# Side work of experts 1 to 7 at other steps, layer 2 over four PSUM tiles, and the second expert's first rows fetched early

## The chip, the cores and the metric

The kernel runs on one core of a Trainium2 chip. Its time is the device time of one execution in microseconds (us); the number compared is the median of several executions. TensorE (PE in the profile) multiplies, VectorE (DVE) and ScalarE (ACT) read PSUM and work on SBUF, GpSimd (POOL) does element work and issues indirect DMAs, SyncE (SP) issues plain DMAs.

## The reference

```python
scores = scale * q @ k.T                      # 8 batches, 8 heads, 576 x 64
thresh = scores.max(-1) - tau                 # tau 0.02
attn = softmax(where(scores >= thresh, scores, -1e9)) @ v
x = attn.reshape(4608, 512)
noisy = x @ w_gate + log1p(exp(x @ w_noise)) * noise
top2 = the two largest of 8 per token; gates = softmax over them
for e in range(8):
    h = maximum(x[rows of e] @ w1[e], 0)      # 512 -> 1024
    out[rows of e] += gate * (h @ w2[e])      # 1024 -> 512
```

Everything is fp32. A matmul operand is split into a rounded high part and the rest (hi and lo), and each product is made of three matmuls (hi by hi, hi by lo, lo by hi).

## The kernel before

**Two halves.** The first 690 us or so are attention, batch by batch, with expert 0 started inside its end. Experts 1 to 7 follow, one after the other. The text is about them and about the seam between expert 0 and expert 1.

**Rows of an expert.** Gating writes, for each expert, a table of its tokens (up to 1188 slots, `slot_table`). An expert reads its table, gathers its rows from `x_rows` in blocks of 128 with indirect DMAs of POOL (`gather2`, L1155), writes each block back to a DRAM buffer `stage` (`bounce2`, SP, L1164), reads it in another layout with four DMAs (`load2`, SP, L1173, into two alternating buffers that the rows call n_zeros and n_xg), and turns it with four DVE transposes (`turn2`, L1182). `EARLY` gives expert 0 a table in two parts: the first 24 blocks of 32 slots hold tokens of batches 0 to 5 only and can be read before the last batches are gated.

**Two phases for an expert.** `PAIRS` cuts the slots into 640 (phase p=0) and 548 (p=1). Layer 1 is Strassen-like: for each of four column units u, seven products k, written here as (k,u), of six matmuls each (`product`, L1239), 28 products in a phase. They accumulate in three PSUM tiles for x, y, z, named by `bank1`: x is tp0 or tp1 by u's parity, y is tp2, z is tp3. `evict` empties them: copies on ACT (L1255), adds on DVE (L1258), then relu into hi (ACT, L1262) and lo (DVE, L1263). x of unit u is thus free again only after relu lo of (4,u), two units on.

**Layer 2.** p=0 has five `plain` tiles of 128 tokens (24 matmuls each, L1317, emptied by ACT L1308); p=1 has two plain tiles and `wide2`, four column parts c of 24 matmuls each (L1332), which DVE transposes out of PSUM (L1339). All take `self.bank(False)`, which rotates over four halves of two tiles of 1024 columns, sp0 and sp1, in the order sp0, sp1, sp0, sp1. Waits between engines are kept by whole tile, so two halves of one tile count as one.

**The order** is written by hand. `STEPS` lists the steps of PE in a phase: 28 products, two "old" steps (the end of the layer 2 before) and, from place 28 on, "new" steps, the first of its own layer 2; then the rest of layer 2. After each step come its evictions, then the side work listed for that step in `run`: `split1` (w1hi on ACT, L1125, w1lo on DVE, L1130) and `sum1` (POOL, L1113) make expert n's w1 operands, `w2hi` (ACT, L1139) and `w2lo` (DVE, L1144) those of w2, `turns` the row turns and loads, `sums` the differences of rows (DVE, L1193) and the split of the row operands X (ACT L1212, DVE L1217). w1, w2 raw values come by SP (L1103, L1135) into four buffers. Each engine runs its list in order.

**The seam.** `START` places expert 0's steps inside attention's last pairs. Its third group (`first[2]`, 14 blocks) and its wide2 run in `steps0`, where before also all of expert 1's first rows are gathered, bounced, loaded and turned, landing in `R0` (buffers qr0, qr1, xl).

Of the kernel before, what the change touches and what calls it, by code (L numbers as in the profile page):

```python
# [39 lines left out]
EARLY = (GROUPS[0] + GROUPS[1],)  # L40
# [8 lines left out]
NEW = ("B", "T", "t", "t5", "G", "Y", "q", "R0", "S", "X", "W", "V", "H")  # L49
# [678 lines left out]
class Experts:  # L728


    def __init__(self, tc, const, work, psum, state, w1, w2, out, x_dram, table, stage):
# [82 lines left out]
        for i, place in enumerate(("qr0", "qr1", "xl")):  # L814
            lay(("R0", i), place, 0, 512)
# [360 lines left out]
    def turn2(self, e, p, i):  # L1176
# [122 lines left out]
    def plain(self, e, t, col, m, order):  # L1299
# [3 lines left out]
        ps = self.bank(False)  # L1303
# [16 lines left out]
    def wide2(self, e, k, col, n, order, last):  # L1320
# [44 lines left out]
    def phase(self, e, p, side1, side2):  # L1365
        second = self.second_steps(e, p)
# [23 lines left out]
        assert not at, sorted(at)  # L1390

    def run(self, count):
        nc = self.nc
# [210 lines left out]
```

## Time and profile before

| what | us |
|---|---|
| median of 3 runs (range 1498.17 to 1506.39) | 1499.37 |
| the profiled execution | 1513.85 |
| its span, first to last instruction | 1512.1 |
| PE busy in it | 1424.1 (94%) |
| DVE, ACT, POOL busy | 1061.1, 856.1, 754.2 |
| mean granted TensorE clock | 0.983 of full |

The profiled execution is 1.0% above the median of the runs; 1.75 us of it lie outside the span. A row of the timeline gives start, length, engine, line, operation, tile written and tiles read, and in square brackets how long the engine had been idle and what ended that. A matmul row's length includes its pipeline tail: the next one starts before it ends, so what a matmul costs is the distance of two starts.

### The profile page before, as it was taken

To read this page: it belongs to the slowest core of one execution; us is meant where nothing else is said; L and a number is where in the kernel's file an instruction comes from. 1 tells how busy PE (TensorE), PEld (TensorE's weight loads), DVE (VectorE), ACT (ScalarE), POOL (GpSimd) and SP (SyncE) were. 2 spreads that over 40 slices of the span, in tenths; PEclk is the share of its full clock that TensorE was granted. 3 is DMA by queue.
4 is the path that set the end of the run, shared out by engine and by line. 5 is a ranking of instruction groups with operands and counts; after the bars stand their busy time and mean duration, and the time that the engine had idled before them with its cause. 6 is when DMAs were issued, how large, how long until landed. Compare 5 with 4: busy or idle time off the path is not lost.

```text
span 1512.1 us, 27923 instructions
## 1 busy us (share of the span) xinstructions
PE 1424.1 (94%) x9086; PEld 1159.8 (77%) x9086; DVE 1061.1 (70%) x2853; ACT 856.1 (57%) x1808; POOL 754.2 (50%) x1149
## 2 busy tenths in 40 slices
PE   8999999999999998989698999899898998998997
PEld 6776667676777766879588888888887887888885
DVE  7888888888888888634766657658658557666640
ACT  7888878888888886312445434435434434443441
POOL 4347565756565667234554444543543552552512
PEclk9999999999999999999899999999999999999999
DMA  7677677777777674346355556555554653663622
GB/s 197 184 195 186 194 180 195 180 204 177 207 178 190 139 211 140 75 109 167 104 128 153 146 99 169 126 117 140 129 142 111 147 135 97 153 153 79 139 29 31
DMA packets 189282, 220.60 MB, mean 146 GB/s; under 512 B 64212, under 2 KB 112300, under 8 KB 188112
## 3 DMA queue, kind: packets, MB, share of 16 engines
q1 hardware_dynamic: 161936, 178.91, 42.5%
q0 software_dynamic: 27200, 39.88, 15.3%
q8 instruction: 74, 1.21, 0.3%
q14 instruction: 72, 0.59, 0.1%
HBM read 103.25 MB, written 60.61 MB: 108 GB/s over the span
## 4 chain that ended last, share of the span: by engine, by line
PE 66%; DVE 10%; issue 9%; ACT 6%; DMA 4%; POOL 3%; SPq 1%; POOLq 0%; DVEq 0%; ACTq 0%
PE m_tp L1239 14%; PE m_sp L1317 13%; PE tp L397 11%; PE tp L331 9%; PE sp L283 9%; PE m_sp L1332 3%; PE m_sp L1000 2%; DVE n_pt L1130 2%; PE tp L417 1%; DVE n_p L1217 1%; DVE n_qr L1258 1%; DMA slot_table<-pay,sl 1%; PE tp L416 1%; POOL out L1021 1%; DMA out<-n_y,sx 1%
## 5 line engine op out<-in xcount | busy, mean ns | idle before, releaser
L296 ACT ACTIVATE e<-ns,nm 128x576 f32<-128x576 f32 x288 | 223.3, 776 | 43.2 <-DVE ns L294 34.3
L319 DVE SCALAR_TENSOR_TENSOR p<-ns,thr,e 128x576 f32<-128x576 f32 x256 | 221.8, 866 | 22.6 <-ACT thr L304 20.7
L294 DVE TENSOR_SCALAR_CACHE_REDUCE ns<-sp 128x576 f32<-128x576 f32 x288 | 214.3, 744 | 18.2 <-PE sp L283 13.0
L1021 POOL DMA_INDIRECT out<-n_y,sx x52 | 82.1, 1579 | 243.2 <-ACT n_y L1308 238.0
L331 PEld LDWEIGHTS tp<-ident,p 128*128 128x128 f32 x1024 | 110.3, 143 | 99.7 <-ACT ot L403 18.3
L334 ACT ACTIVATE pt<-tp 128x512 f32<-128x512 f32 x256 | 150.7, 589 | 55.6 <-PE tp L331 46.1
L397 PE MATMUL tp<-pt,vt 128*64 128x256 f32 (+1 forms) x1024 | 175.6, 427 | 0.0
L331 PE MATMUL tp<-ident,p 128*128 128x128 f32 x1024 | 167.6, 286 | 0.0
L283 PE MATMUL sp<-ks,qh 128*128 128x288 f32 x496 | 159.8, 336 | 5.4 <-DVE ns L294 4.8
L1258 DVE TENSOR_TENSOR n_qr<-m_tp,n_qr 128x320 f32<-128x320 f32 (+1 forms) x168 | 77.0, 461 | 115.2 <-PE m_tp L1239 103.7
L283 PE MATMUL sp<-ks,ql 128*128 128x288 f32 x496 | 138.4, 296 | 0.0
L1239 PE MATMUL m_tp<-n_p,n_pt 128*128 128x274 f32 (+1 forms) x700 | 117.0, 303 | 12.7 <-ACT n_qr L1255 8.1
L1255 ACT ACTIVATE n_qr<-m_tp 128x320 f32<-128x320 f32 (+1 forms) x168 | 67.7, 411 | 107.0 <-PE m_tp L1239 103.6
L213 POOL TENSOR_TENSOR lok<-kr,hik 128x640 fp32r<-128x640 f32 x31 | 56.9, 1834 | 140.5 <-ACT hik L212 139.2
L1239 PEld LDWEIGHTS m_tp<-n_p,n_pt 128*128 128x128 f32 x700 | 100.9, 188 | 19.4 <-ACT n_qr L1255 11.3
L1308 ACT ACTIVATE n_y<-m_sp,gw 128x512 f32<-128x512 f32 (+1 forms) x52 | 35.5, 685 | 130.2 <-PE m_sp L1317 102.7
L1021 POOL DMA_INDIRECT out<-n_y,ix x60 | 97.5, 1625 | 16.2 <-issue 13.3
L640 POOL DMA_INDIRECT slot_table<-pay,sl x80 | 88.2, 1102 | 33.7 <-DVE m_vt L881 16.5
L283 PEld LDWEIGHTS sp<-ks,qh 128*128 128x128 f32 x496 | 93.8, 189 | 7.7 <-DVE ns L294 5.1
L283 PEld LDWEIGHTS sp<-ks,ql 128*128 128x128 f32 x496 | 94.4, 190 | 0.0
L1239 PE MATMUL m_tp<-n_vt,n_pt 128*128 128x320 f32 (+1 forms) x364 | 89.4, 301 | 4.4 <-issue 3.3
L397 PEld LDWEIGHTS tp<-pt,vt 128*64 128x64 f32 x1024 | 56.7, 135 | 42.4 <-issue 27.8
(539 smaller groups left out, 3884.2 us busy)
## 6 DMA issues: line engine op xcount, KB each, us to landing
qh<-hiq SPq DMA_DIRECT2D x124, 144.0 KB
ql<-loq SPq DMA_DIRECT2D x124, 144.0 KB
n_raw<-w SPq DMA_DIRECT2D x56, 256.0 KB
kr<-k SPq DMA_DIRECT2D x32, 320.0 KB
out<-zeros SPq DMA_DIRECT2D x19, 512.0 KB
qr<-q SPq DMA_DIRECT2D x32, 288.0 KB
vt<-v SPq DMA_DIRECT2D x8, 1152.0 KB
n_zeros<-stage SPq DMA_DIRECT2D x140, 64.0 KB
```

What stands on the lines that cost most here:

```text
L283: nc.tensor.matmul(o, q_, k_, start=(i == 0), stop=(i == len(parts) - 1))
L294: nc.vector.tensor_scalar(ns, sp[:, :, 0:HALF], -1.0 / math.sqrt(D), None, op0=ALU.mult, op1=ALU.min, accum_out=nm)
L296: nc.scalar.activation(e, ns, AF.Exp, bias=nm, scale=-1.0)
L319: nc.vector.scalar_tensor_tensor(p, ns, thr, e, op0=ALU.is_le, op1=ALU.mult, accum_out=ssum[n][:, c:c + 1])
L331: nc.tensor.transpose(tp[:, kt, :], p[:, 128 * kt:128 * kt + 128], ident)
L334: nc.scalar.activation(pt[n][:, s, :, c0:c0 + 128], tp, AF.Copy)
L397: nc.tensor.matmul(o[64 * s:64 * s + 64, 0:c1 - c0], w, x, start=(kt == 0), stop=(kt == 4))
L640: st = nc.gpsimd.indirect_dma_start(out=table, out_offset=bass.IndirectOffsetOnAxis(ap=d["sl"][0:m, i, c:c + 1], axis=0), in_=d["pay"][0:m ...
L1021: st = self.nc.gpsimd.indirect_dma_start(out=out, out_offset=bass.IndirectOffsetOnAxis(ap=idx, axis=0), in_=y, in_offset=None, compute_op= ...
L1239: nc.tensor.matmul(ps[:, 0:n], w[a[0]][hw][:, 128 * (a[1] + c):128 * (a[1] + c) + 128], s[hx][:, c0 + c, t0:t0 + n], start=(first and i == ...
L1258: return lambda: nc.vector.tensor_tensor(to, ps, to, op=ALU.add)
L1317: nc.tensor.matmul(ps[0:m], x[:, col:col + m], y, start=(i == 0 and j == 0), stop=(i == 7 and j == 2))
```

## The change

1. `EARLY` holds for expert 1 too: its table also comes in two parts, and 768 of its slots are filled from batches 0 to 5. Its five first blocks are gathered, bounced and partly loaded and turned in `START` (new entries tok1, ix1, gd, bd, ld, td); `steps0` keeps only three turns, one load, the sums and w1. The `R0` buffers are gone; the rows land in buffers of expert 0's rows. This adds 5 DMAs to SP and 10 small instructions to DVE.
2. Layer 2 takes its tiles from a list, `spot`: sp, the other sp, tp2, tp3, sp, the other sp, the first 512 columns of each. x of unit u is tp0, tp1, sp{1-lead}, tp0 for u = 0 to 3.
3. Side work moves by some steps. The order of PE's steps, the matmuls and their number stay.

```diff
-EARLY = (GROUPS[0] + GROUPS[1],)
+EARLY = (GROUPS[0] + GROUPS[1],) * 2
...
+    gc=(16, 16, 16, 17), bc=(16, 16, 16, 17), lc=(17, 17, 18, 20), tc=(19, 20, 21, 22), tok1=-18, ix1=1,
+    gd=(1, 2, 18, 18, 19), bd=(3, 4, 19, 19, 20),
+    ld=(22, 22, 23, 23), td=(23, 23))
...
     def bank1(self, name, u):
-        place = {"x": f"tp{u % 2}", "y": "tp2", "z": "tp3"}[name]
+        place = {"x": ("tp0", "tp1", f"sp{1 - self.lead}", "tp0")[u], "y": "tp2", "z": "tp3"}[name]
...
+    def spot(self):
+        return self.arena[self.spots.pop(0)][:, 0:512] if self.spots else self.bank(False)
...
-            ps = self.bank(False)
+            ps = self.spot()
...
     def phase(self, e, p, side1, side2):
+        lead = self.lead
+        pair = [f"sp{lead}", f"sp{1 - lead}"]
+        self.spots = pair + ["tp2", "tp3"] + pair
...
+        self.lead = 1 - lead if p == 0 else lead
...
+            self.spots = ["sp0", "sp1", "tp0", "tp1", "sp0"]
...
-        for s, f in (rows(1, 0, (0, 0, 0, 3, 3), (2, 2, 3, 5, 6), (4, 4)) + turns(1, 0, (6, 7, 12, 13, 20), (6, 7, 13))
-                     + sums(1, 0, 21) + [(0, call(self.w1load, 1, 0))] + sum1(1, 0, 6) + split1(1, 0, (8, 9, 10))
+        for s, f in (turns(1, 0, (1, 1, 4), (1,), 2) + sums(1, 0, 6) + [(0, call(self.w1load, 1, 0)), (1, call(self.w1load, 1, 1))]
+                     + sum1(1, 0, 4) + split1(1, 0, (13, 14, 15))
...
-                s, v = [], (2, 6, 8, 11, 14, 17, 20, 23)
+                s, v = [], (4, 6, 11, 13, 18, 20, 25, 27)
...
-                + [(a + 2, call(self.w2load, e, 4 + i)) for i, a in enumerate(v[:4])] + turns(e, 1, (25, 27), (26, 29)),
-                turns(e, 1, (5, 7, 13), (6,), 2) + sums(e, 1, 14) + [(4, call(self.tokens, n, 0)), (30, call(self.index, n, 0))]
+                + [(a + 2, call(self.w2load, e, 4 + i)) for i, a in enumerate(v[:4])],
+                turns(e, 1, (1, 2, 8, 9, 15), (2, 3, 9)) + sums(e, 1, 16) + [(4, call(self.tokens, n, 0)), (30, call(self.index, n, 0))]
...
-                rows(n, 0, (1, 2, 3, 4, 5), (12, 13, 14, 15, 16), (18, 19)) + split1(n, 0, (9, 10, 13)) + sum1(n, 1, 12)
-                + [(16, call(self.w1load, n, 2))] + split1(n, 1, (17, 18, 20)) + [(22, call(self.w1load, n, 3))]
-                + sum1(n, 2, 22) + split1(n, 2, (25, 26, 28)) + sum1(n, 3, 30) + turns(n, 0, (25, 27), (26, 29)),
-                turns(n, 0, (5, 7, 13), (6,), 2) + sums(n, 0, 14) + split1(n, 3, (4, 5, 6))
-                + [(a, call(self.w2load, n, i)) for i, a in enumerate((8, 9, 14, 15))])
+                rows(n, 0, (1, 2, 3, 4, 5), (12, 13, 14, 15, 16), (18, 19)) + split1(n, 0, (6, 11, 13)) + sum1(n, 1, 13)
+                + [(16, call(self.w1load, n, 2))] + split1(n, 1, (18, 20, 25)) + [(28, call(self.w1load, n, 3))]
+                + sum1(n, 2, 22) + split1(n, 2, (27,)),
+                turns(n, 0, (4, 5, 9, 10, 15), (5, 6, 10)) + sums(n, 0, 16) + split1(n, 2, (None, 2, 3))
+                + sum1(n, 3, 4) + split1(n, 3, (7, 8, 11))
+                + [(a, call(self.w2load, n, i)) for i, a in enumerate((6, 6, 14, 14))])
```

Three places show how instructions stand now. First DVE in p=1 of an expert, from the relu lo of (4,2) (the first row) to that of (7,3) (the last row of each piece). The two L1258 rows are the adds of (3,3) and (7,3); n_pt are w1 lo parts, the four transposes one turned block of rows. The same functions stand 11 to 16 lines further down now. Before:

```order
L1263 SCALAR_TENSOR_TENSOR n_e_10156<-m_tp_9744,n_ns_10155 128x274
L1130 TENSOR_TENSOR n_pt_10166<-n_xl,n_pt_10166 128x512
L1130 TENSOR_TENSOR n_pt_10166<-n_nz,n_pt_10166 128x256
L1182 STREAM_TRANSPOSE n_kr_9895<-n_xg_9860 128x128
L1182 STREAM_TRANSPOSE n_kr_9897<-n_xg_9860 128x128
L1182 STREAM_TRANSPOSE n_hiq_9899<-n_xg_9860 128x128
L1182 STREAM_TRANSPOSE n_loq_9901<-n_xg_9860 128x128
L1258 TENSOR_TENSOR n_qr_9759<-m_tp_9801,n_qr_9759 128x274
L1263 SCALAR_TENSOR_TENSOR n_xr_10157<-n_qr_9759,n_xr_10157 128x274
L1130 TENSOR_TENSOR n_pt_10166<-n_raw_9767,n_pt_10166 128x512
L1258 TENSOR_TENSOR n_qr_9761<-m_tp_9769,n_qr_9761 128x274
L1263 SCALAR_TENSOR_TENSOR n_e_10159<-n_qr_9761,n_e_10158 128x274
```

Now:

```order
L1279 SCALAR_TENSOR_TENSOR n_e_10171<-m_sp_9049,n_ns_10170 128x274
L1274 TENSOR_TENSOR n_qr_9952<-m_tp_9885,n_qr_9952 128x274
L1141 TENSOR_TENSOR n_pt_10181<-n_raw_9813,n_pt_10181 128x512
L1279 SCALAR_TENSOR_TENSOR n_xr_10172<-n_qr_9952,n_xr_10172 128x274
L1274 TENSOR_TENSOR n_qr_9953<-m_tp_9798,n_qr_9953 128x274
L1279 SCALAR_TENSOR_TENSOR n_e_10174<-n_qr_9953,n_e_10173 128x274
```

Ahead of the add of (3,3) there stood two w1 parts and four transposes, and they are gone from there; one part and the relu lo of (3,3) stand between the two adds as before.

Second, DVE behind the last rows of that phase: the end of the X split (n_p, n_xr) and the transposes of wide2's parts c = 0 and 1 and 2 (L1339, now L1355). Before:

```order
L1217 TENSOR_TENSOR n_p<-n_loq_9901,n_p 128x640
L1217 TENSOR_TENSOR n_xr_9938<-n_qr_9759,n_vt_10035 128x640
L1339 STREAM_TRANSPOSE n_y_10659<-m_sp_9008 128x4x32
L1339 STREAM_TRANSPOSE n_y_10534<-m_sp_9008 128x4x32
L1339 STREAM_TRANSPOSE n_y_10572<-m_sp_9008 128x2x32
L1339 STREAM_TRANSPOSE n_y_10659<-m_sp_9033 128x4x32
L1339 STREAM_TRANSPOSE n_y_10534<-m_sp_9033 128x4x32
L1339 STREAM_TRANSPOSE n_y_10572<-m_sp_9033 128x2x32
L1339 STREAM_TRANSPOSE n_y_10659<-m_sp_9008 128x4x32
```

Now:

```order
L1355 STREAM_TRANSPOSE n_y_10674<-m_tp_9848 128x4x32
L1355 STREAM_TRANSPOSE n_y_10537<-m_tp_9848 128x4x32
L1355 STREAM_TRANSPOSE n_y_10583<-m_tp_9848 128x2x32
L1229 TENSOR_TENSOR n_p<-n_loq_9775,n_p 128x640
L1229 TENSOR_TENSOR n_xr_9978<-n_qr_9952,n_vt_9977 128x640
L1355 STREAM_TRANSPOSE n_y_10674<-m_tp_9885 128x4x32
L1355 STREAM_TRANSPOSE n_y_10537<-m_tp_9885 128x4x32
L1355 STREAM_TRANSPOSE n_y_10583<-m_tp_9885 128x2x32
L1355 STREAM_TRANSPOSE n_y_10674<-m_sp_9014 128x4x32
```

The parts c = 0, 1, 2 came out of two tiles, the third out of the first one's again; they come out of three. The last X parts stand behind c = 0 instead of ahead of it.

Third, SP behind expert 0's third group, where expert 1's blocks are loaded (stage is the DRAM buffer, n_raw, n_hik, n_lok are raw w1). Now:

```order
L1176 DMA stage<-m_p 128x512 x3
L896 DMA ti_76<-slot_table 32x26 x4
L900 DMA ti_76<-slot_table 4x2 x4
L950 DMA m_zeros<-stage 32x2x128 x4
L1185 DMA n_xg_9732<-stage 32x4x128 x4
L1185 DMA n_zeros<-stage 32x4x128 x4
L1185 DMA n_xg_9732<-stage 32x4x128 x4
L1185 DMA n_zeros<-stage 32x4x128 x4
```

Before, behind the same load of m_zeros, the last of expert 0's third group:

```order
L949 DMA m_zeros<-stage 32x2x128 x4
L1103 DMA n_raw_9765<-w 128x512
L1103 DMA n_raw_9767<-w 128x512
L1164 DMA stage<-n_qr_9759 128x512
L1164 DMA stage<-n_qr_9761 128x512
L1164 DMA stage<-n_xl 128x512
```

Three bounces of expert 1 moved ahead of that load, and its first four block loads follow at once.

## Rows read from the trace of the kernel before

**Rows 1.** The page, part 1: busy time, share of the span and instructions of each engine.

```profile
PE 1424.1 (94%) x9086; PEld 1159.8 (77%) x9086; DVE 1061.1 (70%) x2853; ACT 856.1 (57%) x1808; POOL 754.2 (50%) x1149
```

**Rows 2.** Busy time of each engine (instructions in brackets), granted clock, DMA share and GB/s in a stretch of one expert's length, from p=1 of expert 2 to p=1 of expert 3.

```profile
909.50:1018.60 109.10, 101.83 (x601) 91.76 (x600) 72.46 (x174) 47.16 (x101) 52.00 (x59) 0.98 0.55 132
```

**Rows 3.** What PE waited for in experts 1 to 7 (738 us to the end), by line waiting and line waited for: us in total, times, longest.

```profile
PE m_tp L1239 <- DVE n_qr L1258: 13.8, 7, 2.3
PE m_tp L1239 <- ACT n_qr L1255: 10.7, 15, 1.5
PE m_sp L1332 <- DVE n_y L1339: 10.5, 6, 1.8
PE m_tp L1239 <- DVE n_ns L1263: 5.0, 8, 0.8
PE m_tp L1239 <- issue: 4.3, 10, 0.8
PE m_tp L1239 <- DVE n_ptr L1263: 4.1, 8, 0.6
```

**Rows 4.** Timeline around (4,3) in p=1 of one expert: PE first, then DVE.

```profile
931.08 0.85 PE L1317 MATMUL m_sp<-n_pr,n_ns 128*128 128x512 f32 x3
934.18 0.39 PE L1239 MATMUL m_tp<-n_vt,n_xr 128*128 128x274 f32 x1 [2.24 <-DVE n_qr L1258]
...
930.04 0.50 DVE L1182 STREAM_TRANSPOSE n_kr<-n_xg 128x128 f32<-128x128 f32 x2
...
932.57 1.20 DVE L1130 TENSOR_TENSOR n_pt<-n_raw,n_pt 128x512 fp32r<-128x512 f32 x1
933.69 0.43 DVE L1258 TENSOR_TENSOR n_qr<-m_tp,n_qr 128x274 f32<-128x274 f32 x1
```

**Rows 5.** PE busy (instructions), granted clock, DMA share and GB/s in six stretches of 3.5 us, one in each of experts 1 to 6: the first, and the sum over the six.

```profile
826.00:829.50 3.50, 3.50 (x12) 0.53 0.00 0
...
sum 21.00, PE 21.00; mean PE 3.50
```

**Rows 6.** Timeline at wide2 of the same expert: PE at the start of c = 2, and DVE.

```profile
953.29 0.68 PE L1332 MATMUL m_sp<-n_qh,n_pt 128*128 128x292 f32 x3 [1.75 <-DVE n_y L1339]
...
947.96 0.82 DVE L1217 TENSOR_TENSOR n_p<-n_kr,n_p 128x640 fp32r<-128x640 f32 x1
948.69 0.82 DVE L1217 TENSOR_TENSOR n_p<-n_hiq,n_p 128x640 fp32r<-128x640 f32 x1
...
950.16 0.48 DVE L1193 TENSOR_TENSOR n_qr<-n_hiq,n_qr 128x320 f32<-128x320 f32 x1
950.57 0.48 DVE L1193 TENSOR_TENSOR n_qr<-n_loq,n_qr 128x320 f32<-128x320 f32 x1
...
952.60 1.16 DVE L1339 STREAM_TRANSPOSE n_y<-m_sp 128x128 f32<-128x128 f32 x6
```

**Rows 7.** Timeline of PE at the start of (1,3) in p=1.

```profile
922.79 0.53 PE L1239 MATMUL m_tp<-n_p,n_xr 128*128 128x274 f32 x2 [0.79 <-DVE n_ns L1263]
```

**Rows 8.** Timeline of the seam from expert 0 to expert 1: SP, DVE, PE.

```profile
713.08 0.84 SPq L1103 DMA_DIRECT2D n_raw<-w  x2
714.02 1.85 SPq L1173 DMA_DIRECT2D n_zeros<-stage  x4
...
720.82 0.50 DVE L1182 STREAM_TRANSPOSE n_kr<-n_zeros 128x128 f32<-128x128 f32 x2 [4.64 <-DMA n_zeros<-stage]
...
728.36 1.10 PE L1332 MATMUL m_sp<-m_qh,m_pt 128*128 128x292 f32 x3 [9.95 <-DVE m_y L1339]
```

**Rows 9.** Busy time of each engine, granted clock (behind the five engines), DMA share and GB/s in two stretches of the seam.

```profile
720.40:728.36 7.96, 0.00 (x1) 0.00 (x1) 7.54 (x17) 1.31 (x2) 3.60 (x4) 0.50 0.19 62
728.36:734.10 5.74, 5.74 (x23) 5.74 (x24) 5.67 (x9) 3.40 (x6) 0.00 (x0) 0.50 0.01 1
```

**Rows 10.** Timeline of the last block's load and turn in p=1 of two experts: SP's four issues and the first two of DVE's transposes.

```profile
936.94 1.73 SPq L1173 DMA_DIRECT2D n_zeros<-stage  x4
...
940.25 0.51 DVE L1182 STREAM_TRANSPOSE n_kr<-n_zeros 128x128 f32<-128x128 f32 x2 [0.46 <-DMA n_zeros<-stage]
...
1045.94 3.06 SPq L1173 DMA_DIRECT2D n_zeros<-stage  x4
...
1050.57 0.50 DVE L1182 STREAM_TRANSPOSE n_kr<-n_zeros 128x128 f32<-128x128 f32 x2 [1.78 <-DMA n_zeros<-stage]
```

**Rows 11.** Timeline at the start of a p=0: PE at (1,1), ACT's copy of it, PE at (6,1).

```profile
964.28 1.04 PE L1239 MATMUL m_tp<-n_p,n_pt 128*128 128x320 f32 x6
...
968.29 0.44 ACT L1255 ACTIVATE n_qr<-m_tp 128x320 f32<-128x320 f32 x1 [1.56 <-PE m_tp L1239]
...
968.78 0.41 PE L1239 MATMUL m_tp<-n_vt,n_pt 128*128 128x320 f32 x1 [0.82 <-issue]
```

**Rows 12.** Timeline of expert 0's third group: POOL's gather, SP's last load, DVE's turn and split, PE's first matmul on it.

```profile
659.60 0.98 POOL L929 DMA_INDIRECT m_p<-x_rows,sx  x1 [11.75 <-issue]
...
677.87 1.73 SPq L949 DMA_DIRECT2D m_zeros<-stage  x4
...
681.07 0.63 DVE L961 STREAM_TRANSPOSE m_loq<-m_zeros 128x64 f32<-128x64 f32 x4 [0.46 <-DMA m_zeros<-stage]
682.18 0.42 DVE L964 TENSOR_TENSOR m_xr<-m_loq,m_vt 128x256 fp32r<-128x256 f32 x1 [0.48 <-ACT m_vt L963]
...
687.97 0.35 PE L979 MATMUL m_tp<-m_vt,m_xr 128*128 128x420 f32 x1
```

More of the change, by code (lines that the diff above doesn't have):

```diff
@@ L48 @@
 PLACES = 4
-NEW = ("B", "T", "t", "t5", "G", "Y", "q", "R0", "S", "X", "W", "V", "H")
+NEW = ("B", "T", "t", "t5", "G", "Y", "q", "S", "X", "W", "V", "H")
 UNITS = range(4)
@@ L739, in __init__ @@
         self.xt, self.ht, self.wraw, self.wt, self.tok = {}, {}, {}, {}, {}
+        self.rows, self.held, self.spots = {}, {}, []
         self.spacer = const.tile([1, 1], F32, name="spacer1")
@@ L813, in __init__ @@
                 lay((n, i), place, 0, 512)
-        for i, place in enumerate(("qr0", "qr1", "xl")):
-            lay(("R0", i), place, 0, 512)
         lay(("S", 0), "xl", 0, 512)
@@ L1077, in start @@
         add(d["ix"], self.index, 0, 0)
+        add(d["tok1"], self.tokens, 1, 0)
+        add(d["ix1"], self.index, 1, 0)
+        for i in range(5):
+            add(d["gd"][i], self.gather2, 1, 0, i)
+            add(d["bd"][i], self.bounce2, 1, 0, i)
         for e, g, n in ((0, 0, "a"), (0, 1, "b"), (0, 2, "c")):
@@ L1080, in start @@
                 for i in range(2):
-                    add(d["tokb"][i], self.tokens, i, 1 - i)
-                    add(d["ixb"][i], self.index, i, 1 - i)
+                    add(d["tokb"][i], self.tokens, i, 1)
+                    add(d["ixb"][i], self.index, i, 1)
             for i in range(-(-GROUPS[g] // 4)):
@@ L1096, in start @@
                 add(d["l2"][i + 3 * g], self.store, 1)
+        for n, f in (("ld", self.load2), ("td", self.turn2)):
+            for i in range(2):
+                add(d[n][i], f, 1, 0, i)
+        for i in range(2):
+            add(d["ld"][2 + i], self.load2, 1, 0, 2 + i)
         return s
@@ L1146, in landing @@
     def landing(self, e, p, i):
-        return self.buf("R0", i % 3) if (e, p) == (1, 0) else self.buf("H", *((3, 0), (3, 1), (6, 0), (7, 0), (7, 1))[i])
+        return self.buf(*(("r0", 0), ("r0", 1), ("r", 1), ("r", 2), ("r", 0))[i]) if (e, p) == (1, 0) else self.buf("H", *((3, 0), (3, 1), (6, 0), (7, 0), (7, 1))[i])
     def gather2(self, e, p, i):
@@ L1154, in gather2 @@
         self.fresh = True
-        self.nc.gpsimd.indirect_dma_start(out=self.landing(e, p, i)[0:m, 0:512], out_offset=None, in_=self.x[0],
+        self.nc.gpsimd.indirect_dma_start(out=self.landing(e, p, i)[0:m, 0:512], out_offset=None,
+                                          in_=self.x[(e, p) == (1, 0)],
                                           in_offset=bass.IndirectOffsetOnAxis(ap=self.tok[e][2][0:m, t:t + 1], axis=0))
@@ L1390, in phase @@
         assert not at, sorted(at)
+        self.lead = 1 - lead if p == 0 else lead
     def run(self, count):
         nc = self.nc
-        self.rows, self.held, self.now, self.pending = {}, {}, 0, []
+        self.now, self.pending = 0, []
         def call(f, *a):
@@ L1399, in split1 @@
         def split1(e, u, s):
-            return ([(x, call(self.w1hi, e, u, n)) for x, n in zip(s, "asb")]
-                    + [(x + 1, call(self.w1lo, e, u, n)) for x, n in zip(s, "asb")])
+            return ([(x, call(self.w1hi, e, u, n)) for x, n in zip(s, "asb") if x is not None]
+                    + [(x + 1, call(self.w1lo, e, u, n)) for x, n in zip(s, "asb") if x is not None])
         def sum1(e, u, s):
@@ L1440, in run @@
         assert not at, sorted(at)
-        self.old = []
+        self.old, self.lead = [], 1
         for e in range(1, E):
```

11 lines of the change are left out of this document (5 added, 6 removed).

## The prediction

> **What bounds the kernel now.** The page first [rows 1]: PE is busy 94% of the span and the next engine, DVE, 70%, so what can be won lies in PE's holes and in stretches where its clock is not full. One expert of the steady part takes 109.1 us, with PE busy 101.8 and a mean clock of 0.98 [rows 2]. The table of PE's waits over experts 1 to 7 then says whom the holes wait for [rows 3]; see in it that four of the six lines name DVE, together 33.4 us in 29 waits, and that the other two (ACT's copy L1255, and "issue"), 15.0 us in 25 waits, are smaller and more scattered. The timelines say why DVE is late at each; the seam from expert 0 to expert 1 is one more and the largest hole [rows 8].
>
> **Part by part. The wait at (4,3) in p=1.** (4,3) adds onto the x of unit 3, so it waits until DVE has read it for (7,3). DVE does that at 933.69, because it came out of row transposes at 930.04 and then had a w1 part of 1.20 us ahead of the add; PE stands 2.24 us [rows 4]. The line is 13.8 us in 7 waits [rows 3]. In the new order two w1 parts and four transposes are gone from ahead of the adds. By such rows (0.50 us for two transposes, so some 0.8 for four that overlap; a part no shorter than the 0.43 of an add and no longer than 1.20) that is 1.7 to 3.2 us of DVE's queue, an estimate, as much as the hole, and PE has three layer 2 steps, 2.1 us, between (7,3) and (4,3). I take the wait as gone: 13.8 us. Nothing else was queued as late there: (7,3)'s copy on ACT is ahead of it.
>
> **wide2.** c = 2 stands 1.75 us until DVE has transposed c = 0 out of the same tile [rows 6]; 10.5 us in 6 waits [rows 3]. DVE is at the X split then (0.74 us each from row to row) and stays there in the new order; it even does c = 0 no sooner. But c = 2 goes to another tile whose last reader, ACT's eviction of a plain tile, is two parts back. Gone: 10.5 us. What is late next is the next phase's (2,0), which needs tp2, where c = 0 now is, only some 11 us later.
>
> **x of units 2 and 3.** (1,3) in p=1 waits 0.79 us for the relu lo of (4,1) [rows 7], and (1,2) in p=0 likewise for (4,0): 5.0 and 4.1 us [rows 3]. With unit 2 in an sp tile and unit 3 in tp0, the readers to wait for are a unit further back. Gone: 9.1 us.
>
> **The size of a hole.** The idle column is counted from the modelled end of the matmul ahead, which lies about 0.16 us beyond where the next would have started (0.39 long, 0.23 apart in layer 2). 29 waits by 0.16 are 4.6 us more. Holes together: 38.0 us.
>
> **The clock.** Behind these holes PE's clock was granted at half: six stretches of 3.5 us at 0.51 to 0.53 [rows 5], five behind (4,3), one behind a wide2 wait. 21.0 us of work at about half speed lose 10.3 us, against what full clock would do. [...] This is the softest term: the profiled execution is 14.5 us above the median, and these stretches may not stand in every run. Its bounds are 0 and 10.3.
>
> **The seam.** In wide2 of expert 0 PE stands 9.95 us, since DVE, ahead of the transposes of c = 0, waits 4.64 us for a block of expert 1's rows and then works off the sums [rows 8]. The clock falls to half meanwhile, and the 5.74 us of work behind run at 0.50 [rows 9], which loses 2.9. Now the five blocks are turned before the third group's layer 1 is through, and wide2's parts use four tiles. With the same sum rule that is 9.95 + 0.16 + 2.9 = 13.0 us. Against it stands POOL: two gathers of about 1.3 us now stand among the slot_table scatters that expert 0's third group waits for, and three bounces, which wait for three more gathers, stand on SP ahead of that group's last load. That load was issued at 677.87, turned at 681.07 and split by 682.6, and PE needed it at 687.97 [rows 12], so 5.4 us were to spare. The two gathers cost 2.6, the bounces 1.5 of issue and 0 to 3 of waiting: 4.1 to 7.1 in all, so 0 to 1.7 us late. I take 1.
>
> **New waits on DVE.** In p=1 blocks 2 to 4 are turned 4 or 5 steps of 0.7 us behind their loads, where 7 to 9 stood between before. From the first of four issues to the turn it took 3.3 us at 936.94 and 4.6 at 1045.94, with DVE idle 0.46 and 1.78 [rows 10]. In p=1 the last load also stands behind two loads of w2 of 256 KB. DVE may so be 1 to 3 us late before the sums. What it has to do from there to the last X part that product (2,0) needs is one turn 0.8, six differences and two more of 0.41, six splits of 0.74 and c = 0's transposes 0.6, together 9.1 us. PE has 96 matmuls of 0.135 us less two steps, (1,0), and an old step until then, 13.5. The cover is 4.4 us, so I cost this at nothing; if it is gone, PE stands at (2,0). For p=0 more layer 2 lies behind (24 matmuls of 0.23 for each of three tiles). The moved w1 and w2 splits have one answer each: all are still ahead of their first product by a unit. I allow 3 us for small things in seven experts, between 0 and 8.
>
> Here the Trainium skill speaks against the change. In the trace a block's load issued right behind w1 loads (713.08, then 714.02) reached DVE at 720.82 [rows 8], 6.8 us from its first issue against 3.3 to 4.6 [rows 10]. "DMA: Bandwidth & Descriptors", section "Queues, rings and completion order", says that each DMA engine consumes the descriptors of one ring in order, so a small load behind large ones of the same queue waits for theirs. That row agrees with it; by it the last load of p=1 would be late by more than my 1 to 3 us, and the sum would be that of the first rival.
>
> **The sum.** 38.0 + 10.3 + 13.0 - 1 - 3 = 57.3 us off the profiled execution's 1513.85: 1456.6. In the ratio of the median to it (1499.37 / 1513.85) that is 1442.6; I say 1443. The 15.0 us of the other two lines of rows 3 I leave in: at the start of a p=0, ACT's copy of (1,1) starts 3 us after PE's last row of it, with ACT idle, and (6,1) starts behind it [rows 11]; nothing in the change touches that.
>
> **The rivals.** First, slower: the rows of the next expert land late at each seam, as they did at the seam of expert 0. Place: the fifth block in p=1, its load behind two w2 loads, DVE waiting for it with X's split and wide2's transposes behind. It decides from 4.4 us later than the hand sum; below that nothing is lost. The price of the one case seen is 9.95 us of hole and 2.9 of half clock, 12.9; at six seams 77: 1499 - 57 + 77 = 1519. For it: the 4.64 us wait, and a turn now nearer its load. Against it: 4.4 us of cover by the hand sum, where expert 0's seam had the transposes right behind the turn. 4%.
>
> Second: PE's late signals. With the holes closed, PE arrives sooner at places like (6,1) where ACT learned of a finished product 3 us late. If two such waits of about 0.9 us are added in each of 13 phases, 23 us of the gain are lost: 1466. For it: it stands beside POOL's gathers, which stay. Against it: these waits don't follow the holes but the start of a phase. 13%.
>
> Third: the seam gives nothing, since expert 0's third group is late by what the new gathers and bounces cost and PE's clock falls there. Then the 13.0 are gone and some 5 more: 1461. 12%.
>
> Fourth: the change doesn't do what it says, because the profiled holes are mostly the profiler's and runs without it have few. Then little moves, about 1495. Against it: 94% busy and 7 equal holes in 7 experts. 3%.
>
> Fifth: the 15.0 us left in go as well, in part: 1432. 5%.
>
> **How the numbers follow.** The forecast has the rest, 63%: 1443, from 1435 (no small losses) to 1453 (no clock term). The range reaches to the fifth case below and the second and third above, 1430 to 1467, which holds 93% by these cases; I leave it so, since the clock term and the third case could come together. A measurement of this kernel tells about 0.5%, 7.5 us, from no change. Faster by more than that: 0.63 + 0.13 + 0.12 + 0.05 = 0.93. Within: 0.03. Slower: 0.04.
>
> **What would show it.** In the profile after: no DVE line above 1 us in total among PE's waits, for products or for wide2; mean clock of an expert at 1.00 where it was 0.98; an expert in about 101.5 us instead of 109.1; wide2 of expert 0 without a hole; DVE idle for block loads in p=1 by 1 to 3 us without PE standing at (1,0) or (2,0). Wrong I am if PE stands at (2,0) of a p=0, or if the two remaining lines grow by over 10 us.

## The result and the profile after

The changed kernel takes **1443.51 us** (median of 4 runs, 1442.19 to 1447.06), beside 1500.69 for the kernel before (4 runs, 1498.17 to 1506.39): a ratio of 0.9618, 95% interval 0.9584 to 0.9651. The forecast was 1443. The profiled execution took 1442.19 us (span 1440.5), which is 1.3 us below its median, where that of before was 14.5 us above. So the two traces differ by 71.66 us, and the medians by 57.2.

The page of the changed kernel, part 1, answers to [rows 1]:

```profile
PE 1401.6 (97%) x9086; PEld 1149.0 (80%) x9086; DVE 1044.8 (73%) x2863; ACT 856.8 (59%) x1808; POOL 756.1 (52%) x1149
```

Busy time by stretch follows (columns as in rows 2): a stretch of experts 2 and 3 as in [rows 2], and all of experts 1 to 7, from their first product to their last matmul. After:

```profile
870.00:970.00 100.00, 99.03 (x604) 90.94 (x603) 70.36 (x174) 47.22 (x102) 52.26 (x59) 1.00 0.61 144
729.40:1430.40 701.00, 692.94 (x4175) 632.04 (x4176) 467.96 (x1160) 322.62 (x693) 356.01 (x396) 1.00 0.58 135
```

Experts 1 to 7 in the kernel before:

```profile
738.30:1502.00 763.70, 714.08 (x4177) 639.79 (x4176) 482.46 (x1157) 323.70 (x693) 351.76 (x394) 0.99 0.52 124
```

The work of one expert (some 600 instructions of PE) now takes 100 us and not 109. Over seven experts the stretch is 62.7 us shorter. PE's idle time in it fell from 49.6 us (763.70 less 714.08) to 8.1, which is 41.6; its busy time fell by 21.1, and the granted clock rose to 1.00. The rest of the 71.66 lies ahead: expert 1's first product starts at 729.38 instead of 738.31, 8.9 us earlier.

What PE waited for from 690 us to the end after the change (us in total, times, longest), to be held against [rows 3]:

```profile
PE m_tp L1255 <- ACT n_qr L1271: 6.0, 8, 1.8
PE m_tp L980 <- ACT m_vt L964: 2.4, 1, 2.4
PE m_tp L1255 <- DVE n_y L1355: 2.0, 4, 0.7
PE m_tp L1255 <- DVE m_y L1355: 1.2, 1, 1.2
```

All four DVE lines of rows 3 are gone. A new one, 2.0 us in 4 waits, has come. ACT's line and "issue" together are down from 15.0 to 6.0; about 1.0 of that fall are six waits of 0.16 to 0.18 us at (1,3), x of unit 3, that rows 3 have under "issue".

DVE itself waits more than before. Its waits for blocks of rows over experts 1 to 7 (us in total, times, longest), after:

```profile
DVE n_kr L1194 <- DMA n_zeros<-stage: 63.5, 26, 7.3
...
DVE n_kr L1194 <- DMA n_xg<-stage: 19.7, 11, 2.6
...
DVE n_kr L1194 <- DMA ti<-slot_table: 7.8, 2, 4.1
```

The same of the kernel before:

```profile
DVE n_kr L1182 <- DMA n_zeros<-stage: 31.1, 13, 6.7
```

That is 83.2 us in 37 waits, and 91.0 in 39 with the last line, instead of 31.1 in 13: those two waits also stand ahead of the turn of a block (the fourth of a p=0), and the profile puts them down to another DMA. In each p=1 of experts 1 to 6 DVE now waits 4.7 to 5.5 us for blocks, where it was 0.5 to 1.8; the rest is in p=0. The timeline of one p=1 of the changed kernel (the expert after that of rows 4) shows where: SP's issues of the last three blocks and the loads of w2 among them (n_raw), DVE's turns of those blocks and its transposes of c = 0 and 1 of wide2, then PE at (5,0), the product behind (2,0).

```profile
1012.02 2.72 SPq L1185 DMA_DIRECT2D n_zeros<-stage  x4
1014.84 1.83 SPq L1185 DMA_DIRECT2D n_xg<-stage  x4
1016.77 0.95 SPq L1146 DMA_DIRECT2D n_raw<-w  x2
1017.82 1.82 SPq L1185 DMA_DIRECT2D n_zeros<-stage  x4
...
1016.38 0.51 DVE L1194 STREAM_TRANSPOSE n_kr<-n_zeros 128x128 f32<-128x128 f32 x2 [2.04 <-DMA n_zeros<-stage]
...
1020.20 0.51 DVE L1194 STREAM_TRANSPOSE n_kr<-n_xg 128x128 f32<-128x128 f32 x2 [2.02 <-DMA n_xg<-stage]
...
1023.09 0.51 DVE L1194 STREAM_TRANSPOSE n_kr<-n_zeros 128x128 f32<-128x128 f32 x2 [1.42 <-DMA n_zeros<-stage]
...
1030.92 0.63 DVE L1355 STREAM_TRANSPOSE n_y<-m_tp 128x128 f32<-128x128 f32 x3
...
1032.19 0.81 DVE L1229 TENSOR_TENSOR n_xr<-n_qr,n_vt 128x640 fp32r<-128x640 f32 x1
1032.92 0.63 DVE L1355 STREAM_TRANSPOSE n_y<-m_tp 128x128 f32<-128x128 f32 x3
...
1033.61 0.56 PE L1255 MATMUL m_tp<-n_p 128*128 128x320 f32 x2 [0.73 <-DVE n_y L1355]
```

DVE stands 2.04 + 2.02 + 1.42 = 5.48 us in this phase. The three blocks are turned 4.4, 5.4 and 5.3 us behind their first issues (rows 10 had 3.3 and 4.6). PE stands only 0.73 us for it: (5,0) writes tp3 and starts 0.06 us after DVE has read c = 1 out of tp3 (1032.92 + 0.63).

The seam, to be held against [rows 8, 9, 12]: timeline of the changed kernel with a gather of expert 1's rows on POOL, SP's last load for expert 0's third group, DVE's turn of it, PE's wait for that group and PE at expert 1's first product.

```profile
676.63 1.05 POOL L1166 DMA_INDIRECT m_p<-x_rows,sx  x1 [4.15 <-DMA stage<-m_p]
...
684.27 2.02 SPq L950 DMA_DIRECT2D m_zeros<-stage  x4
...
688.74 0.62 DVE L962 STREAM_TRANSPOSE m_loq<-m_zeros 128x64 f32<-128x64 f32 x4 [8.17 <-DMA m_zeros<-stage]
...
689.86 0.72 PE L980 MATMUL m_tp<-m_vt,m_xr 128*128 128x420 f32 x1 [2.36 <-ACT m_vt L964]
...
729.38 0.56 PE L1255 MATMUL m_tp<-n_p 128*128 128x320 f32 x2 [1.20 <-DVE m_y L1355]
```

The 9.95 us in wide2 are gone. The third group's last load is issued 6.4 us later than before (684.27 against 677.87), so PE stands 2.36 us for it, and 1.20 at expert 1's first product.

### The profile page after: what moved, and what is told of

Same layout as the page of the kernel before. It is cut to its first block, busy times and chain, and to the rows that moved or that the text cites. A ratio compares the mean times of both kernels' runs of the same rounds, so it can differ in the third digit from the quotient of the medians.

```text
span 1440.5 us, 27937 instructions
## 1 busy us (share of the span) xinstructions
PE 1401.6 (97%) x9086; PEld 1149.0 (80%) x9086; DVE 1044.8 (73%) x2863; ACT 856.8 (59%) x1808; POOL 756.1 (52%) x1149
## 4 chain that ended last, share of the span: by engine, by line
PE 60%; DVE 11%; DMA 9%; issue 8%; POOL 5%; ACT 4%; SPq 2%; POOLq 0%; DVEq 0%; ACTq 0%
PE m_tp L1255 13%; PE tp L399 9%; PE m_sp L1333 9%; PE tp L333 8%; PE sp L285 7%; PE m_tp L1333 5%; DMA slot_table<-pay,sl 2%; PE m_sp L1255 2%; DMA n_zeros<-stage 2%; POOL out L1022 1%; SPq L1185 1%; DMA kr<-k 1%; DVE n_pt L1141 1%; PE tp L419 1%; PE m_sp L980 1%
## 5 line engine op out<-in xcount | busy, mean ns | idle before, releaser
L321 DVE SCALAR_TENSOR_TENSOR p<-ns,thr,e 128x576 f32<-128x576 f32 x256 | 222.5, 869 | 22.4 <-ACT thr L306 21.1
L1022 POOL DMA_INDIRECT out<-n_y,sx x52 | 86.0, 1655 | 187.9 <-ACT n_y L1324 180.4
L215 POOL TENSOR_TENSOR lok<-kr,hik 128x640 fp32r<-128x640 f32 x31 | 57.3, 1848 | 140.1 <-ACT hik L214 139.7
L1274 DVE TENSOR_TENSOR n_qr<-m_tp,n_qr 128x320 f32<-128x320 f32 (+1 forms) x154 | 69.8, 460 | 50.4 <-PE m_tp L1255 49.8
L1255 PE MATMUL m_tp<-n_p,n_pt 128*128 128x320 f32 (+1 forms) x616 | 101.3, 301 | 0.5 <-ACT n_qr L1271 0.5
L1255 PEld LDWEIGHTS m_tp<-n_p,n_pt 128*128 128x128 f32 x616 | 88.9, 188 | 1.9 <-ACT n_qr L1271 1.1
L1271 ACT ACTIVATE n_qr<-m_tp 128x320 f32<-128x320 f32 (+1 forms) x140 | 57.6, 413 | 44.4 <-PE m_tp L1255 29.3
L1324 ACT ACTIVATE n_y<-m_sp,gw 128x512 f32<-128x512 f32 (+1 forms) x36 | 24.8, 688 | 96.9 <-PE m_sp L1333 67.7
L1224 ACT ACTIVATE n_vt<-n_qr 128x640 fp32r<-128x640 f32 (+1 forms) x42 | 29.3, 701 | 87.5 <-DVE n_qr L1205 87.5
```

The lines of the kernel that those rows point to most:

```text
L321: nc.vector.scalar_tensor_tensor(p, ns, thr, e, op0=ALU.is_le, op1=ALU.mult, accum_out=ssum[n][:, c:c + 1])
L1022: st = self.nc.gpsimd.indirect_dma_start(out=out, out_offset=bass.IndirectOffsetOnAxis(ap=idx, axis=0), in_=y, in_offset=None, compute_op= ...
L1255: nc.tensor.matmul(ps[:, 0:n], w[a[0]][hw][:, 128 * (a[1] + c):128 * (a[1] + c) + 128], s[hx][:, c0 + c, t0:t0 + n], start=(first and i == ...
L1274: return lambda: nc.vector.tensor_tensor(to, ps, to, op=ALU.add)
```

## The experiments

Three series, each on one chip; each kernel is compared with the kernel before in its own series, since that took 1516.66 us in the first (e1 to e4), 1523.82 in the second (e5 to e8) and 1501.76 in the third (e9 to e12).

**The kernel before once more** (no edit). 

> The kernel before once more, for a second trace. By the prediction's terms DVE's four lines among PE's waits stand again at 33 us within 2, since they follow from the order; what the first profiled execution had over the median (14.5 us) lies elsewhere, in the waits for ACT and issue and in attention. By the fourth rival the DVE lines are much smaller in an execution near the median, under 20 us.

One run: 1519.21 us. PE's waits for DVE stand there again: 13.5 us in 6 for L1258, 10.5 in 6 for wide2, 4.9 and 4.1 for the relus. So the holes of rows 3 belong to the program and not to one execution of it. The half clock behind them does less so: four stretches of 3.4 us in experts 1 to 7 here, two behind (4,3) and two behind a wide2 wait of 1.75 us, where [rows 5] had six.

**The PSUM tiles alone**, put into the kernel before with its old steps:

```diff
-        place = {"x": f"tp{u % 2}", "y": "tp2", "z": "tp3"}[name]
+        place = {"x": ("tp0", "tp1", f"sp{1 - self.lead}", "tp0")[u], "y": "tp2", "z": "tp3"}[name]
...
-            ps = self.bank(False)
+            ps = self.spot()
...
+        self.spots = pair + ["tp2", "tp3"] + pair
```

> The kernel before with the PSUM places of the change alone (spot, lead, bank1). If the terms add: the holes of wide2 and of the x tiles go, 10.5 + 9.1 and 2 of tails, and part of expert 0's wide2 hole, 3 to 7: 25 to 29 us less than before, and the (4,3) hole of 2.2 us with its half clock stays. If instead DVE is simply late and PE waits at the next place for it: 5 to 12 us less, with new DVE holes at the phase starts.

1490.20 us, ratio 0.9838 (0.9794 to 0.9881). PE's waits (columns as above):

```profile
PE m_tp L1244 <- DVE n_qr L1263: 16.5, 6, 2.8
PE m_tp L1244 <- ACT n_qr L1260: 14.7, 23, 1.8
PE m_tp L1244 <- DVE m_y L1344: 11.5, 1, 11.5
```

wide2 and the relu lines are gone, (4,3) has grown from 13.5 to 16.5, and the seam's hole has only moved, from wide2 to expert 1's first product, where it is 11.5 us. So the tiles take away two of the three causes and leave the third, which is one of order.

**The new steps alone**, with the old PSUM tiles:

```diff
-                + sum1(n, 2, 22) + split1(n, 2, (25, 26, 28)) + sum1(n, 3, 30) + turns(n, 0, (25, 27), (26, 29)),
-                turns(n, 0, (5, 7, 13), (6,), 2) + sums(n, 0, 14) + split1(n, 3, (4, 5, 6))
+                + sum1(n, 2, 22) + split1(n, 2, (27,)),
+                turns(n, 0, (4, 5, 9, 10, 15), (5, 6, 10)) + sums(n, 0, 16) + split1(n, 2, (None, 2, 3))
+                + sum1(n, 3, 4) + split1(n, 3, (7, 8, 11))
```

(and the other lists of experts 1 to 7 as in the change). 

> The kernel before with the side work of experts 1 to 7 at the new steps alone. If the terms add: the (4,3) hole goes, 13.8 and 1 of tails, and five of six half clock stretches, 8.6: 21 to 25 us less than before; wide2 and x holes stay, wide2's as long or some tenths longer, and one half clock stretch may now stand behind wide2. If DVE is simply late: 5 to 10 us less, with wide2's holes over 3 us.

1535.17 us, ratio 1.0123 (1.0085 to 1.0161): **slower**, by 1.2%. PE's waits:

```profile
PE m_sp L1332 <- DVE n_y L1339: 38.4, 6, 6.8
PE m_sp L1332 <- DVE m_y L1339: 12.5, 2, 10.8
PE m_tp L1239 <- DVE n_ptr L1263: 9.5, 14, 0.9
...
PE m_tp L1239 <- DVE n_qr L1258: 1.7, 5, 0.4
```

The order does what was forecast at (4,3): 13.5 us have become nothing, for the 1.7 us of that line stand at (4,0). But wide2's wait has grown from 10.5 to 38.4 us, again in 6 waits: DVE comes to the transposes of c = 0 later, because it waits for the last blocks, and PE's third part needs the tile that c = 0 stands in.

**The early fetch alone**, with the old steps of experts 1 to 7 and the old tiles:

```diff
-EARLY = (GROUPS[0] + GROUPS[1],)
+EARLY = (GROUPS[0] + GROUPS[1],) * 2
...
+    gd=(1, 2, 18, 18, 19), bd=(3, 4, 19, 19, 20),
+    ld=(22, 22, 23, 23), td=(23, 23))
```

> The kernel before with the early fetch of expert 1's rows alone (EARLY, START, steps0). By the sum of the prediction 12 us less, of which the trace of the changed kernel showed 9 between the first matmul of expert 0's second half and expert 1's start; by the third rival nothing or 5 us more. In the steady part nothing changes: one expert 109 us.

1522.42 us, ratio 1.0035 (1.0017 to 1.0053): 5.8 us slower. PE's waits for the end of expert 0:

```profile
PE m_sp L1348 <- DVE m_y L1355: 5.3, 1, 5.3
...
PE m_tp L980 <- ACT m_vt L964: 3.0, 1, 3.0
```

The hole in wide2 is halved and not gone, since c = 2 still waits for c = 0, and PE stands 3.0 us for the third group. That group starts 6.0 us later than in e1 (698.14 against 692.19), and from there to expert 1's first product only 4.1 us are won. Alone, with the old tiles and the old order, the early fetch gives nothing.

**The change again, in the second series** (no edit). 

> The changed kernel on the chip of this job. If its gain is the interaction seen between the parts (PSUM places alone about 25 us less, order alone about 18 more, early fetch alone about 5 more), the whole is again 3.5 to 4.5% under the kernel before of the same job, although its parts alone sum to about nothing. Its DVE again waits 80 us for block loads in experts 1 to 7 (31 in the kernel before).

1462.81 us, ratio 0.9594 (0.9556 to 0.9632). The ratio holds; the waits don't all. ACT's copy is 13.4 us in 20 waits here, against 6.0 in 8 above: in each p=1 of experts 1 to 6 PE stands 0.6 to 1.1 us at (6,1) and twice 0.4 after it, where the first trace has one wait of 0.4 or none. The new DVE line is 2.7 in 5, four at (5,0) and one of 0.26 at (2,0). One stretch of 3.4 us at half clock stands in expert 1, behind a wait of 1.83 us at (6,1).

**Without the tiles for x of units 2 and 3**, all else as changed:

```diff
-        place = {"x": ("tp0", "tp1", f"sp{1 - self.lead}", "tp0")[u], "y": "tp2", "z": "tp3"}[name]
+        place = {"x": f"tp{u % 2}", "y": "tp2", "z": "tp3"}[name]
```

> The changed kernel with x of unit u back in tp0 or tp1 by parity, the rest as changed. If the x terms are worth what the waits of the kernel before say: 9 us and 2 of tails more than the changed kernel, as waits for DVE's relu lo at (1,2) and (1,3). If DVE is now so much less loaded there that PE does not wait: under 4 us.

1477.38 us, ratio 0.9710 (0.9671 to 0.9749), so 14.6 us behind the change in its series. PE's waits for the relus are back:

```profile
PE m_tp L1255 <- DVE n_ptr L1279: 7.7, 11, 0.9
PE m_tp L1255 <- DVE n_ns L1279: 2.1, 11, 0.2
```

9.8 us of holes in 22 waits; with five more at the same products, which the profile puts down to other names, 11.4 in 27. With 0.16 us of tail each, as in the prediction, that is 15.7. The four times of each kernel lie within 7 to 8 us, so 14.6 is known to some 5 us.

**The old steps of w2's splits in p=0:**

```diff
-                s, v = [], (4, 6, 11, 13, 18, 20, 25, 27)
+                s, v = [], (2, 6, 8, 11, 14, 17, 20, 23)
```

> The changed kernel with the w2 splits of p=0 back at steps 2, 6, 8, ... . Tells what took away the two holes of 0.8 to 1.0 us at (6,1) and (3,1) at the start of a p=0, which the prediction left in. If it was the w2 split and its load at step 4: they are back, 1.7 us in each of 6 or 7 phases, 10 to 12 us more than the changed kernel. If it was that PE now arrives there later behind its wait at (2,0): 0 to 3 us more.

1465.82 us, ratio 0.9622 (0.9587 to 0.9658), 3.0 us more than the change with intervals that overlap: no difference that this can tell. ACT's line stands at 12.5 us in 20 waits, as in e5 (13.4 in 20). At (6,1) and (3,1) of p=0 in experts 2 to 7 there are two waits of 0.5 and 0.6 us, where the kernel before has ten. So it is not the place of w2's splits that took these holes away.

**w2's loads behind the last block, and three bounces later:**

```diff
-    gd=(1, 2, 18, 18, 19), bd=(3, 4, 19, 19, 20),
+    gd=(1, 2, 18, 18, 19), bd=(3, 4, 21, 21, 21),
...
-                + [(a, call(self.w2load, n, i)) for i, a in enumerate((6, 6, 14, 14))])
+                + [(a, call(self.w2load, n, i)) for i, a in enumerate((11, 11, 14, 14))])
```

> The changed kernel with the first two w2 loads of p=1 issued behind the last block load (places 11, 11 for 6, 6) and the three late bounces of expert 1 behind expert 0's last load (places 21 for 19, 19, 20). If loads of one queue wait for those ahead: DVE's wait for the last block falls by 1 to 2 us in each p=1, the 0.3 to 0.7 us holes at (2,0) go (2 us) and the 2.4 us hole at expert 0's third group goes: 2 to 6 us less than the changed kernel. If the wait is the loads' own landing time: DVE waits as long as before and only the third group's hole goes, 0 to 3 us less.

1463.87 us, ratio 0.9605 (0.9571 to 0.9640): no gain over the change. DVE's waits for blocks fell from 90.9 us (65.1 and 25.8) to 80.7 (55.0, 18.8 and 6.9 that are put down to slot_table). All of the fall is in p=1, from 31.4 to 20.3 us. (5,0) no longer waits, and neither does the third group. But PE's waits are now:

```profile
PE m_tp L1255 <- ACT n_qr L1271: 15.8, 26, 1.8
PE m_tp L1255 <- issue: 4.7, 6, 1.0
```

That is 20.5 us against 14.5 (13.4 and 1.1) in e5. In p=0 of each of experts 2 to 7 PE now stands at (6,1), (3,1) or both, 0.3 to 1.0 us, as rows 11 show it in the kernel before; in e5 only one of these phases had such a wait. So about 6 us came in while about 3 went, those at (5,0) and the third group's 0.7.

**The change a third time** (no edit). 

> The changed kernel again, as the measure for the other three on this chip: 3.8 to 4.1% under the kernel before.

1444.24 us, ratio 0.9624 (0.9594 to 0.9655).

**Without the four tiles for layer 2**, all else as changed:

```diff
-            ps = self.spot()
+            ps = self.bank(False)
```

(at both places). 

> The changed kernel with layer 2 back on the rotating halves of sp0 and sp1, x banks and order as changed. If the spots are what hides DVE's longer wait for block loads: wide2's c = 2 waits 6 to 7 us in six experts, 38 to 45 us more than the changed kernel, with half clock behind. If the x banks did most: under 20 us more.

1499.71 us, ratio 0.9988 (0.9971 to 1.0005): with this one thing taken out, **nothing of the 57 us is left**. PE's waits:

```profile
PE m_sp L1348 <- DVE n_y L1355: 38.0, 6, 6.8
...
PE m_sp L1348 <- DVE m_y L1355: 5.3, 1, 5.3
```

The timeline of one of the six holes, DVE first and then PE:

```profile
1039.58 0.51 DVE L1194 STREAM_TRANSPOSE n_kr<-n_zeros 128x128 f32<-128x128 f32 x2 [1.94 <-DMA n_zeros<-stage]
...
1043.96 0.51 DVE L1194 STREAM_TRANSPOSE n_kr<-n_xg 128x128 f32<-128x128 f32 x2 [2.59 <-DMA n_xg<-stage]
...
1046.62 0.50 DVE L1194 STREAM_TRANSPOSE n_kr<-n_zeros 128x128 f32<-128x128 f32 x2 [1.19 <-DMA n_zeros<-stage]
...
1054.44 0.64 DVE L1355 STREAM_TRANSPOSE n_y<-m_sp 128x128 f32<-128x128 f32 x3
...
1055.13 1.10 PE L1348 MATMUL m_sp<-n_qh,n_pt 128*128 128x292 f32 x3 [6.76 <-DVE n_y L1355]
```

And the stretches behind it (columns as in rows 2):

```profile
1055.10:1059.00 3.90, 3.87 (x16) 3.87 (x17) 1.98 (x5) 0.19 (x1) 0.00 (x0) 0.50 0.00 0
1059.00:1064.00 5.00, 5.00 (x31) 5.00 (x31) 0.64 (x3) 0.00 (x0) 0.48 (x1) 0.77 0.00 0
```

DVE waits 5.72 us for blocks, as in the change (5.48), but here PE stands 6.76 us for it, and its clock is at half behind the hole: 3.9 us at 0.50 and 5.0 at 0.77 lose 1.95 + 1.15 = 3.1. Behind the six holes PE works 28.6 us at 0.50 (3.2 to 6.2 each), which loses 14.3. So the six holes and their clock are 38.0 + 14.3 of the 55.5 us between this kernel and e9. The edit also puts expert 0's wide2 back, with holes of 5.3 and 1.5 us where the change has 1.2.

**Tiles and order without the early fetch** (e2 and e3 together):

```diff
-EARLY = (GROUPS[0] + GROUPS[1],) * 2
+EARLY = (GROUPS[0] + GROUPS[1],)
```

(and what hangs on it). 

> The changed kernel without the early fetch: PSUM places and order as changed, START and steps0 as before. If the early fetch costs by itself (as alone, 5 us more than the kernel before) it is 0 to 5 us faster than the changed kernel. If it needs the PSUM places to pay, since expert 0's wide2 then waits for nothing: the hole of 11.5 us at expert 1's first product that stood with the PSUM places alone is back, and it is 8 to 14 us slower.

1447.93 us (1447.26 to 1448.80), ratio 0.9646 (0.9617 to 0.9675), against 1442.19 to 1446.43 for e9 in the same series: 3.7 us between medians. PE at expert 1's first product, and its clock behind that:

```profile
734.50 0.87 PE L1244 MATMUL m_tp<-n_p 128*128 128x320 f32 x2 [10.56 <-DVE m_y L1344]
```

```profile
734.50:740.00 5.50, 5.50 (x21) 5.50 (x22) 5.50 (x15) 2.57 (x6) 3.41 (x3) 0.50 0.27 57
```

The hole of 10.56 us and the half clock are there, about as the prediction priced them, and yet the early fetch wins only 3.7. In the first trace of the change expert 1's first product starts 5.1 us earlier (729.38 against 734.50), since against the hole stand 1.20 us at the same place and a third group that starts 2.8 us later (689.86 against 687.07). Expert 1's p=0 then takes 54.4 us without the early fetch, half clock included, against 56.1 in the change, where PE stands 3.97 us in that phase for ACT's copy.

**The gathers of the next expert later**, put on e8:

```diff
-                rows(e, 1, (1, 2, 3, 4, 5), (12, 13, 14, 15, 16), (18, 19)) + s
+                rows(e, 1, (7, 8, 9, 10, 11), (12, 13, 14, 15, 16), (18, 19)) + s
```

(in p=1 likewise). 

> e8 with the five gathers of each phase at steps 7 to 11 for 1 to 5. If PE's late completions at the start of a phase come from POOL's gathers: the holes at (6,1) and (3,1) of p=0 go from there, 5 to 10 us less than e8, or move later. If they come from something else: they stay, within 3 us of e8.

1444.69 us, ratio 0.9619 (0.9590 to 0.9649), as the change. The holes at (6,1) and (3,1) of p=0 are not there, but (5,0)'s wait is back (2.6 us in 5), and this series had few of those holes anyway (e9: ACT's line 5.6 us in 7). It separates nothing.

## Why the prediction was right, and where its steps were off

The number is right, and the three causes that it named are the ones the runs confirm. But it added its terms as if each stood alone, and they don't.

- **The wait at (4,3), 13.8 us: right.** The new order alone takes it away (e3), the tiles alone leave it (16.5, e2). The line holds six holes of 2.25 us, in the p=1 of experts 1 to 6, and one of 0.29 us at another product, so the fourth rival's "7 equal holes in 7 experts" was misread. That rival is out by the 57 us between the medians.
- **wide2, 10.5 us: right in place, and far too small as a price of the tiles.** Against the old order it is 10.5 us; under the new one it would be 38 (e3, e10). The prediction said that in the new order DVE "even does c = 0 no sooner" and left it there. In fact the order makes that wait 28 us longer, and the tiles hide all of it.
- **x of units 2 and 3, 9.1 us: right as far as the runs tell.** With the tails of its 16 waits it is 11.7, and 1.0 more stood under "issue". Taken out again it costs 14.6 (e6), which is known to some 5 us.
- **The size of a hole and the clock, 4.6 and 10.3 us.** PE's busy time fell by 21.1 in the two traces, where these terms say 14.9. No stretch of experts 1 to 7 is at half clock in the first trace of the change, against six [rows 5], so the clock term stands for this pair of traces. For the program it is less: e1 has four such stretches, which by the same reckoning lose 6.8, and e5, the change again, still has one. The two lines that were left in have 17 waits fewer; if these had tails as well, that is 2.7 more by the same 0.16. The remaining 3.5 I can't place.
- **The seam, 13.0 less 1: too large.** The trace gives 8.9 up to expert 1's first product; taking the early fetch out costs 3.7 (e11). The hole and its clock were priced rightly (10.56 us, then 5.5 us at 0.50). The third group was not: its load moved by 6.4 us, within the 4.1 to 7.1 forecast, but it cost a hole of 2.36, where 1 was taken and 1.7 was the bound, since the load itself also took 4.5 us from its first issue to the turn and not 3.2. And in expert 1's p=0, 1.7 us more are lost. That PE meets ACT's late copies sooner there is argued, not shown.
- **New waits on DVE, "1 to 3 us late", cover 4.4, costed at nothing: the step that failed.** DVE waits 4.7 to 5.5 us in each p=1. The cover is used up and PE does stand, 2.0 us in 4 waits. It stands behind the four p=1 in which DVE waits 5.0 us or more (0.27 to 0.73 us) and not behind the two with 4.7 and 4.9, so the cover of 4.4 was about right and the lateness was mis-sized. And it stands at (5,0) on tp3, behind c = 1, where the prediction looked only at (2,0) on tp2, behind c = 0. The cost of the mistake is 2 us and not more, because c = 0 and c = 2 no longer share a tile. With them sharing one, the same lateness costs 38.0 us of holes and 14.3 of clock (e10).
- **The loads of w2 ahead of the last block.** In e5 that block is turned 5.4 to 6.1 us after its first issue in p=1, where rows 10 had 3.3 and 4.6; with w2's loads moved behind it (e8) it is 4.0 to 4.6, and DVE's waits in p=1 fall by 11 us of 31. Most of the lateness is thus not w2's: the blocks ahead, with no w2 load among them, take 4.4 and 5.4 us as well (first trace), and the turn now stands nearer its load. The Trainium skill ("DMA: Bandwidth & Descriptors", section "Queues, rings and completion order") says that an engine consumes one ring's descriptors in order. The trace agrees in direction. The first rival, 1519 us, had the right mechanism, a late DVE with wide2's transposes behind it, but it comes about where c = 0 and c = 2 share a tile: it is what e3 shows, 1.2% slower than before.
- **The 15.0 us left in** became 6.0 in the profiled execution, 3.97 of them in expert 1, but 14.5 in e5. In one series the fifth rival is half right, in another it isn't. e7 shows that the place of w2's splits is not the cause. In e8 those of p=0 are back where the wait at (5,0) ahead of them is gone. That the one follows from the other, by PE's sooner arrival, is not shown: p=0 of experts 2 and 6 in the first trace has neither wait. Why ACT learns some 3 us late that PE is through with (1,1) [rows 11] stays open; e12 was to tell and did not.

In terms of the profiled executions the sum was too small: 57.3 us forecast against 71.66. Idle time is 41.6 us less, where 33.4 less 3 was forecast; the difference is mostly the 9.0 of the lines left in. The ratio to the median brought the forecast to the right place all the same, because the profiled execution of before lay 14.5 us above its median and that of after did not. What those 14.5 us are, no run here tells; that the forecast meets the median within 1 us is luck.

Of the signs that the prediction named, the clock of 1.00 and an expert of about 101.5 us came (1.00 and 100). A DVE line above 1 us stands all the same. PE at (2,0) of a p=0, the sign of being wrong, does not show in the first trace, but once each in e5 and e11, 0.26 us.

**Alone and together.** Tiles alone -26.5 us, order alone +18.5, early fetch alone +5.8: by that the change would win 2 us. Together they win 57 to 61 in three series. The order takes PE's waits at (4,3) away and makes DVE late; the tiles make that lateness nearly harmless. With the tiles in place the order, 18.5 us slower alone, wins some 29 (ratio 0.9646 in e11 against 0.9838 in e2). The early fetch gives its little with both; with the tiles alone it was not run. No variant beat the changed kernel by more than a measurement can tell.

## What to carry to other kernels

Where work is moved behind a transfer, price it together with whatever frees PE of that engine, here a PSUM tile of its own: a part that is slower when tried alone can be half of the gain. Follow a late engine to every tile that it still has to read, not only to the first that the next phase writes. And where one hole goes another may come (e8), so leaving one part out of the whole says more about its worth than the holes that it names.

## What the runs showed of the hardware

- The same program took 1500.69, 1516.66, 1523.82 and 1501.76 us (medians, kernel before) in four series, a spread of 1.5%, with the ratio of the two kernels at 0.9618, 0.9594 and 0.9624. Times of different series can't be subtracted.
- Which small waits stand in a trace also changes from series to series for one program: ACT's line is 6.0 us in 8 waits, then 13.4 in 20, then 5.6 in 7.
- Half clock stood for 3.4 us behind holes of PE as short as 1.75 us (1169.76 in the kernel before, twice in e1) and 1.83 us (e5), though not behind each hole of that length or of 2.25 us.
- Behind a hole of 6.76 us PE's granted clock was 0.50 for 3.9 us and 0.77 over the next 5.0; behind one of 10.56 us it was 0.50 for 5.5.
